# Gate and up as seven half-size products in a chain of two banks, four down groups, and TensorE's order made from two lanes

## The chip, the core and the metric

The kernel runs on one NeuronCore of a Trainium2 chip. Its engines are TensorE (PE, with the weight loads shown apart as PEld), VectorE (DVE), ScalarE (ACT), GpSimd (POOL) and SyncE (SP), which here only issues DMAs. Each engine works through its own list of instructions in order and waits at semaphores for the others. The metric is device microseconds of the whole program, from DRAM inputs to the DRAM output; lower is better.

## What is computed

A block of layer normalisation, sliding-window attention and a gated feed-forward, whose results are multiplied:

```python
xn = _layernorm(x, axis=-1)                 # x: 2048 tokens x 512
# A: 32 heads of 16, causal window of 256 tokens
qkv = xn @ wqkv; p = softmax(mask(q @ k.T * 16**-0.5)); s = (p @ v) @ wo
# B: feed-forward with F = 1792
gate = xn @ w1;  up = xn @ w3
h = silu(gate) * up
g = silu(h @ w2)
return x + s * g
```

Everything is float32. The kernel multiplies float32 as three float16 products: each operand is cut into a high half and a low half ("hi" and "lo"), and hi x hi, lo x hi and hi x lo are summed in PSUM.

## The kernel before

The 2048 tokens are four tiles `t` of 512, and the 1792 hidden features are 14 blocks `f` of 128. Attention runs in 32 units, each a tile, a group of eight heads and a half of it. A unit is split into batches: score products (`s`, in two double banks of PSUM), masks added by DVE, an exponential on ACT, row maxima for a later unit (`pass1`, on DVE, written to `junk` and `M`), and the products of probabilities and values (`po`, one double bank). These use quarter-size or half-size tiles of TensorE.

The dense work is all that uses the full 128 x 128 array: projections of Q, K and V, gate and up, down, and the output projection (`total`). It shares the last two PSUM banks, `m0` and `m1`, which `bank()` hands out in turn. `spread()` puts dense pieces between the attention batches so that TensorE always has something to do; what is left after the last unit runs at the end.

Gate and up of a block `f` of a tile (`gate_up`, L929) are 24 matmuls of 512 columns: two matrices, four chunks of the 512 features, three half products. ACT takes a tanh of the gate from its bank (L948), DVE makes `(tanh + 1) * gate` (L952) and multiplies by up (L957). Weights of gate and up are cut in tile 0, stored in DRAM as `dW1`, and loaded again for each later tile.

Down is done in groups of blocks, `GROUPS = ((0, 4), (4, 10), (10, 14))`. Tile 0 and the last group of tile 3 use plain matmuls of 512 columns (`down`, L973). The other groups are done by Strassen's scheme: with both operands cut into 2 x 2 squares, seven products of squares of half the size replace eight (`product`, L1025, matmuls of 256 columns). The sums of squares on the left are made by `lefts` (L884, POOL and ACT), those of the weights once in tile 0 (L869 to L880). Each group's result is added to a float32 sum on DVE (L1007, L1053). `combine` (L1057) makes the four result squares from the seven products on POOL. Small fixed pieces (`halves`, L312) run POOL operations as two of 256 columns.

Slots are 46 SBUF buffers handed out by `take` and `give`. Scaling of weights by powers of two is measured in tile 0 (`measure`, L784; `measure_down`, L831).

Two things set the order. TensorE's order is that in which the program is written, since `ORDERED = {ENGINE.PE}`. The other engines' order comes from `listed` (L1543 and after), a list scheduler that plays the program through with a cost for each instruction (`cost`, L1516) and a due time (`deadlines`), and then fixes the order with dependencies. The program calls `tc.manual_schedule(engines=ORDERED)`.

## Time and profile before

| | |
|---|---|
| median of 3 runs | 819.77 us (819.29 to 821.17) |
| the profiled execution | 821.13 us |
| its span, first to last instruction | 819.3 us |
| mean granted clock of TensorE | 0.994 |
| TensorE busy | 797.9 us, 97% |
| DVE busy | 639.2 us, 78% |
| ACT busy | 435.3 us, 53% |
| POOL busy | 358.7 us, 44% |
| DMA | 121.99 MB, 149 GB/s on average |

Busy time of PE is not PE at its peak: a matmul of 512 columns is shown with some 0.38 us, but the next one starts 0.216 us later. So the price of matmuls is read from start to start, that is, from the length of a long row of equal ones. Idle times are put down to the semaphore that came last. The page cuts the span into 40 slices; PE shows nine tenths or more in nearly all of them.

### The profile page before, as it was taken

To read this page: it belongs to the slowest core of one execution; us is meant where nothing else is said; L and a number is where in the kernel's file an instruction comes from. 1 tells how busy PE (TensorE), PEld (TensorE's weight loads), DVE (VectorE), ACT (ScalarE), POOL (GpSimd) and SP (SyncE) were. 2 spreads that over 40 slices of the span, in tenths; PEclk is the share of its full clock that TensorE was granted. 3 is DMA by queue.
4 is the path that set the end of the run, shared out by engine and by line. 5 is a ranking of instruction groups with operands and counts; after the bars stand their busy time and mean duration, and the time that the engine had idled before them with its cause. 6 is when DMAs were issued, how large, how long until landed. Compare 5 with 4: busy or idle time off the path is not lost.

```text
span 819.3 us, 23768 instructions
## 1 busy us (share of the span) xinstructions
PE 797.9 (97%) x9088; PEld 415.8 (51%) x9088; DVE 639.2 (78%) x2044; ACT 435.3 (53%) x659; POOL 358.7 (44%) x556
## 2 busy tenths in 40 slices
PE   8999999699999999999999999999999999999998
PEld 4444444344544554454555555545555555545654
DVE  8898889977897777799778866777878787774535
ACT  6898799555636554443443455534443446544421
POOL 2247646672806433523341752514141456435252
PEclk9999999899999999999999999999999999999999
DMA  9996575268665334545364452426375543224521
GB/s 284 284 296 185 164 215 169 75 197 204 176 179 136 117 103 121 152 144 154 106 189 133 125 142 69 140 72 172 112 185 152 159 146 113 56 90 149 172 65 55
DMA packets 112835, 121.99 MB, mean 149 GB/s; under 512 B 18448, under 2 KB 77008, under 8 KB 112720
## 3 DMA queue, kind: packets, MB, share of 16 engines
q1 hardware_dynamic: 112432, 119.94, 51.2%
q8 instruction: 71, 1.16, 0.6%
q10 hardware_dynamic: 288, 0.52, 0.2%
q14 instruction: 44, 0.36, 0.1%
HBM read 83.76 MB, written 32.37 MB: 142 GB/s over the span
## 4 chain that ended last, share of the span: by engine, by line
PE 83%; DVE 12%; issue 2%; DMA 1%; ACT 1%; DVEq 0%; SPq 0%; ACTq 0%
PE m L937 32%; PE m L1040 9%; PE m L550 9%; PE po L706 8%; PE s L678 5%; PE m L1118 5%; PE m L520 5%; PE m L987 4%; DVE junk L616 3%; PE s L604 3%; DVE s L685 2%; PE po L604 2%; DVE st L422 1%; DMA qa<-dQ 1%; DVE slot L957 1%
## 5 line engine op out<-in xcount | busy, mean ns | idle before, releaser
L688 ACT ACTIVATE pt<-s,es 128x1024 f32<-128x1024 f32 x152 | 167.7, 1113 | 198.0 <-DVE s L685 193.3
L937 PE MATMUL m<-XH,slot 128*128 128x512 f16 x896 | 267.4, 380 | 1.0 <-DVE slot L952 0.8
L316 POOL TENSOR_TENSOR slot<-slot,slot 128x256 f16<-128x256 f32 (+1 forms) x222 | 148.6, 696 | 152.4 <-ACT slot L320 66.6
L937 PEld LDWEIGHTS <-slot 128*128 128x128 f16 x1344 | 124.5, 98 | 152.6 <-issue 12.3
L937 PE MATMUL m<-XL,slot 128*128 128x512 f16 x448 | 169.8, 379 | 0.0
L685 DVE TENSOR_TENSOR s<-s,MK 128x256 f32<-128x256 f32 (+2 forms) x280 | 120.7, 437 | 50.4 <-PE s L678 41.9
L616 DVE CUSTOM_DVE_ANT_0 junk<-s,MW 128x320 bf16<-128x320 f32 x276 | 134.5, 487 | 28.0 <-PE s L604 18.6
L906 POOL TENSOR_TENSOR slot<-slot,slot 128x256 f16<-128x256 f32 x133 | 87.9, 685 | 46.4 <-ACT slot L902 46.3
L1040 PE MATMUL m<-slot,slot 128*128 128x256 f16 x798 | 96.4, 276 | 2.0 <-DVE s L685 1.8
L616 DVE CUSTOM_DVE_ANT_0 junk<-po,MW 128x320 bf16<-128x320 f32 x172 | 84.0, 488 | 10.0
L1040 PEld LDWEIGHTS <-slot 128*128 128x128 f16 x798 | 76.9, 99 | 20.4 <-issue 4.5
L706 PE MATMUL po<-pt,V 64*32 64x320 f32 (+4 forms) x2880 | 78.2, 345 | 0.0
L706 PEld LDWEIGHTS po<-pt,V 64*32 64x32 f32 x2880 | 51.9, 106 | 23.8 <-PE s L604 4.0
L910 POOL TENSOR_TENSOR slot<-slot,slot 128x256 f32<-128x256 f32 x19 | 14.2, 747 | 102.8 <-DVE slot L957 96.5
L678 PE MATMUL s<-qa,KA 50*64 50x320 f16 (+3 forms) x1472 | 58.2, 259 | 1.0 <-ACT pt L688 1.0
L987 PE MATMUL m<-slot,slot 128*128 128x512 f16 x216 | 51.6, 386 | 7.0 <-DVE slot L1007 4.7
L952 DVE SCALAR_TENSOR_TENSOR slot<-slot,m 128x512 f32<-128x512 f32 x56 | 38.3, 683 | 24.0 <-ACT slot L948 23.8
L678 PEld LDWEIGHTS <-KA 50*64 50x64 f16 x1472 | 30.2, 105 | 50.9 <-issue 36.3
L716 ACT COPY os<-po 128x512 f32<-128x512 f32 x32 | 18.7, 585 | 70.2 <-PE po L706 70.2
L948 ACT ACTIVATE slot<-m,sgs 128x512 f32<-128x512 f32 x56 | 38.3, 684 | 32.2 <-PE m L937 31.3
L957 DVE SCALAR_TENSOR_TENSOR slot<-m,slot 128x512 f32<-128x512 f32 x56 | 38.5, 687 | 15.9 <-PE m L937 15.5
L604 PE MATMUL s<-KA,qa 48*64 48x320 f16 (+2 forms) x648 | 45.5, 295 | 1.9 <-DVE M L616 0.7
(170 smaller groups left out, 1137.1 us busy)
## 6 DMA issues: line engine op xcount, KB each, us to landing
slot<-dW SPq DMA_DIRECT2D x88, 256.0 KB
slot<-dR SPq DMA_DIRECT2D x56, 256.0 KB
slot<-in_B_w_dram SPq DMA_DIRECT2D x42, 256.0 KB
dW<-slot SPq DMA_DIRECT2D x32, 256.0 KB
slot<-in_A_x_dram SPq DMA_DIRECT2D x30, 256.0 KB
KA<-dK SPq DMA_DIRECT2D x24, 288.0 KB
dR<-slot SPq DMA_DIRECT2D x49, 128.0 KB
qa<-dQ SPq DMA_DIRECT2D x32, 192.0 KB
```

Source lines behind the costliest of these rows:

```text
L316: op(out[:, c], a[:, c], b[:, c])
L550: nc.tensor.matmul(cell["pp"], a[:, k, c, :], b[:, c, :], start=(c, i) == parts[0][0], stop=(c, i) == parts[-1][-1])
L604: nc.tensor.matmul(s[64 * c:64 * c + 64, r, :n], qa[rows, 2 * p + a, ii * P + 64 * c:ii * P + 64 * c + 64], ka[rows, 2 * p + a, e - n:e], ...
L616: nc.vector.tensor_tensor_reduce(out=junk[:, :n], in0=s[:, r, :n], in1=mask, scale=1.0, scalar=NEG, op0=ALU.add, op1=ALU.max, accum_out=M[ ...
L678: nc.tensor.matmul(s[64 * h:64 * h + 64, r, o:o + 64 * n], ka[rows, 2 * p + a, 64 * (m + 4):64 * (m + 5)], qa[rows, 2 * p + a, 64 * (m + k ...
L685: nc.vector.tensor_add(v, v, MK[:, kind, of:of + n, :].unsqueeze(1).to_broadcast([P, 2 * len(which), n, 64]))
L688: nc.scalar.activation(pt, s, AF.Exp, scale=es)
L706: nc.tensor.matmul(cell["po"][32 * i:32 * i + 32, h, 64 * (m + k):64 * (m + k + n)], V[64 * h:64 * h + 64, (4 * t + m // 2) % VB, hd * VW: ...
L906: nc.gpsimd.tensor_sub(made[:, D + c.start:D + c.stop], raw[:, c], made[:, c])
L937: nc.tensor.matmul(cell[k], w[:, (a * NC + c) * P:(a * NC + c + 1) * P], b[:, c, :], start=c == 0 and i == 0, stop=c == NC - 1 and i == 2)
L987: nc.tensor.matmul(ps, hh[:, a * TW + b * P:a * TW + (b + 1) * P], w[:, c * D:(c + 1) * D], start=f == f0 and i == 0, stop=f == f1 - 1 and ...
L1040: nc.tensor.matmul(ps[:, blk, :], l[:, a * D + q:a * D + q + 128], r[:, 256 * c:256 * c + 256], start=f == f0 and x == 0, stop=f == f1 - 2 ...
```

## The change

**Gate and up of tiles 1 to 3** are done for two blocks at a time (`chain`). The weights of the pair, 512 features x 256 hidden features, and the 512 x 512 tokens of the tile are cut into 2 x 2 squares. Seven products of squares replace eight. Each is 12 matmuls of 256 columns (gate and up, two chunks, three half products) into one bank `[P, 2, 256]` that holds gate and up side by side. The seven go through two banks: `y` takes products 0, 2 and 4, and `x` takes 1, 3, 5 and 6, some of them accumulated on what is there. In between, the bank's state is taken out four times by ACT ("kept", a scaled copy into the float32 tile `cc`) and three times by DVE ("added", a scaled sum into it). The chain comes in four links of 2, 3, 1 and 1 products, and attention batches or other dense pieces are put between them; a rule in `chosen` asks for a filler before the third and the fourth link.

After a chain, tanh is taken from `cc` in SBUF, POOL multiplies gate by up (two operations a block), and one DVE operation finishes the block (`multiplied`).

**Sums of squares.** `combine_tokens` makes four sums of each later tile's tokens on POOL, cut into halves by ACT and POOL. `combine_weights` reads the weights from DRAM a second time, scales them on ACT, adds on POOL, cuts, and stores four sums per pair in `dW1`, which now holds seven squares per pair. The table `COMBOS` says at which block each pair's sums are begun: 5, 8 and 11 of tile 0, and then 0, 2, 4 and 6 of tile 1. Each product's weights (256 KB) are loaded anew, three products ahead.

**Down** has four groups, the last with two blocks. Tile 3 thus has 12 instead of 10 blocks in products. Down pieces that are due go into a list `late` and are taken off by cost (`PACE`), instead of two or three after each block.

**Room.** There are 50 slots, and the QK weights no longer stay in SBUF: they are stored in DRAM (`dWQ`) and loaded again for each later tile and group.

**Order.** TensorE is no longer in the written order. `streams` cuts its instructions into blocks of attention and of dense work (at most six matmuls), two lanes that each keep their order, and `listed` takes from the lane whose turn it is, or from the other if the first would wait more than `GAIN` = 300 ns. Costs and latencies of the scheduler are set anew, and a fault in `box` (what an access covers) is mended.

```diff
-GROUPS = ((0, 4), (4, 10), (10, 14))
+GROUPS = ((0, 4), (4, 8), (8, 12), (12, 14))
...
+CHAIN = ("12 21", "11 11", "s1 t1", "s2 t2", "s4 22", "s3 t3", "22 t4")
+WEIGHTS_AHEAD = 3
+PACE = 16
+COMBOS = {0: 5, 1: 8, 2: 11, 3: 14, 4: 16, 5: 18, 6: 20}
...
-    dW1 = dram.tile([FB, 2, P, 2 * NC * P], F16, name="dW1")
+    dWQ = [[dram.tile([P, 2 * NC * P], F16, name=f"dWQ{g}{k}") for k in range(2)] for g in range(NG)]
+    dW1 = dram.tile([FB // 2, 7, P, 2, 2, 256], F16, name="dW1")
...
+        def sums(k):
+            e, o = raws[k, 0], raws[k, 1]
+            for raw in (o, e):
+                nc.scalar.activation(raw, raw, AF.Copy, scale=pair_scale[:, j, k:k + 1])
+            nc.gpsimd.tensor_add(o[:, two], o[:, one], o[:, two])
+            nc.gpsimd.tensor_sub(o[:, one], e[:, one], o[:, one])
+            nc.gpsimd.tensor_sub(e[:, one], o[:, two], e[:, one])
+            nc.gpsimd.tensor_sub(e[:, two], e[:, two], e[:, one])
...
+    def multiplied(t, f, gate, up):
+
+        sg = take(F32)
+        nc.scalar.activation(sg, gate, AF.Tanh, scale=chain_scale[:, f // 2:f // 2 + 1])
+        halves(nc.gpsimd.tensor_mul, gate, gate, up)
+
+        def product():
+            nc.vector.scalar_tensor_tensor(sg, sg, 1.0, gate, op0=ALU.add, op1=ALU.mult)
+            WHOLE[t, f] = sg
+            finished(t, f)
+        later(1, product)
...
+        def times(p, ps, start):
+            w = WQ.pop((t, j, p))
...
+            for k in range(2):
+                for c in range(2):
+                    for i, (a, b) in enumerate(((0, 0), (1, 0), (0, 1))):
+                        first = k * 512 + a * 256 + c * P
+                        nc.tensor.matmul(ps[:, k, :], w[:, first:first + P], right[b][:, c, :],
+                                         start=start and k == 0 and c == 0 and i == 0, stop=c == 1 and i == 2, skip_group_check=True)
+            give(w)
+            fetch_weights(chains.index((t, j, p)) + 1 + WEIGHTS_AHEAD)
...
+        def kept(f, h, ps):
+            with urgent():
+                nc.scalar.activation(cell[f][:, :, 256 * h:256 * h + 256], ps, AF.Copy, scale=CS)
+
+        def added(f, h, ps):
+            c = cell[f][:, :, 256 * h:256 * h + 256]
+            with urgent():
+                nc.vector.scalar_tensor_tensor(c, ps, CS, c, op0=ALU.mult, op1=ALU.add)
...
+            times(0, cell["y"], True)
+            kept(0, 0, cell["y"])
+            times(1, cell["x"], True)
+            added(0, 0, cell["x"])
...
+            times(2, y, True)
+            kept(1, 1, y)
+            times(3, x, False)
+            times(4, y, False)
+            kept(0, 1, y)
+            added(0, 1, x)
+            done(0)
...
+            times(5, cell["x"], False)
+            added(1, 1, cell["x"])
...
+            times(6, cell["x"], False)
+            kept(1, 0, cell["x"])
+            done(1)
...
+PIECE, GAIN, LEADING, FOLLOW = 6, 300, 8000, 0.0
...
-    with _tile.TileContext(nc) as tc, tc.manual_schedule(engines=ORDERED):
+    with _tile.TileContext(nc) as tc:
```

Three places of the new order matter later. The first is DVE's list where tile 2 is normalised, in the second half of tile 0. L434 to L437 are the small steps of the reciprocal root, L440 centres the tokens, and L1007 adds a down result of tile 0 into its sum, which frees the bank `m1`. Before:

```order
L435 SCALAR_TENSOR_TENSOR sq_2852<-sq_2852,ve_2847 128x4
L436 SCALAR_TENSOR_TENSOR r0_2849<-sq_2852,r0_2849 128x4
L437 TENSOR_SCALAR rs_160<-r0_2849 128x4
L440 TENSOR_SCALAR slot9_2469<-slot9_2469,mv_159,rs_160 128x512
L440 TENSOR_SCALAR slot22_2471<-slot22_2471,mv_159,rs_160 128x512
L1007 SCALAR_TENSOR_TENSOR slot4_1423<-m1_2573,dsc_158,slot4_1423 128x512
```

After, with L1222 for the sum and L452 to L454 for the small steps:

```order
L440 BN_STATS st_3660<-slot11_3404 128x6
L440 BN_STATS st_3674<-slot30_3432 128x6
L1222 SCALAR_TENSOR_TENSOR slot35_1489<-m1_3861,dsc_170,slot35_1489 128x512
L441 BN_AGGR mv_171<-st_3660 128x2
L441 BN_AGGR mv_171<-st_3674 128x2
L445 TENSOR_SCALAR ve_3701<-mv_171 128x4
L448 TENSOR_SCALAR r0_3703<-ve_3701 128x4
L449 TENSOR_SCALAR r0_3703<-r0_3703 128x4
L452 TENSOR_TENSOR sq_3706<-r0_3703 128x4
```

The sum now stands ahead of the whole normalisation instead of behind it; five small steps later the list goes on with masks and maxima, and the rest of the steps follow between them.

The second is DVE's list at one chain of tile 1 (its sixth). L1143 is "added", L646 a row maximum, L715 a mask, L588 the low half of a projection. Before there was no such place; the nearest is a block of gate and up, of which this is the part at the end of tile 3:

```order
L685 TENSOR_TENSOR s_13215<-s_13215,MK_119 128x2x2x64
L952 SCALAR_TENSOR_TENSOR slot40_13212<-slot40_13212,m0_13199 128x512
L1125 SCALAR_TENSOR_TENSOR slot3_13245<-m1_13232,us_4300,slot39_12945 128x256
L1125 SCALAR_TENSOR_TENSOR slot3_13245<-m1_13232,us_4300,slot16_12948 128x256
L957 SCALAR_TENSOR_TENSOR slot40_13212<-m0_13251,slot40_13212 128x512
```

After:

```order
L1143 SCALAR_TENSOR_TENSOR cc_7318<-m0_7317,cc_7318 128x2x256
L715 TENSOR_TENSOR s_7457<-s_7457,MK_120 128x2x2x64
L646 ISA junk_7475,M_7294<-s_7470,MW_112 128x320
L646 ISA M_7294 128x1
L646 ISA junk_7477,M_7294<-s_7470,MW_112 128x320
```

and then, after two more maxima:

```order
L646 ISA junk_7486,M_7294<-po_7479,MW_112 128x320
L646 ISA M_7294 128x1
L588 SCALAR_TENSOR_TENSOR slot35_7452<-m1_7438,slot35_7452 128x512
L1143 SCALAR_TENSOR_TENSOR cc_7388<-m0_7317,cc_7388 128x2x256
L715 TENSOR_TENSOR s_7515<-s_7515,MK_120 128x4x64
```

The two sums that free the same bank `m0` for the chain's next products have a batch's four maxima between them.

The third is POOL's list at the very end. `combine` of tile 3 adds the seven products, which before are in slots 0, 2, 7, 24, 25, 44 and 15 and after in slots 6, 16, 21, 25, 36, 38 and 39; `on<-on,rb` divides the last attention group by its row sums, which come by DMA. Before:

```order
L316 TENSOR_TENSOR slot0_12195<-slot0_12195,slot7_11828 128x256
L316 TENSOR_TENSOR slot44_12039<-slot44_12039,slot0_12195 128x256
L316 TENSOR_TENSOR slot45_13407<-slot6_13388,slot45_13407 128x256 x2
L316 TENSOR_TENSOR slot25_12278<-slot25_12278,slot0_12195 128x256
L316 TENSOR_TENSOR on_13047<-on_13047,rb_13328 128x256 x2
L316 TENSOR_TENSOR slot4_13495<-on_13047,slot4_13495 128x256 x2
L316 TENSOR_TENSOR slot2_11811<-slot2_11811,slot44_12039 128x256
L316 TENSOR_TENSOR slot24_12058<-slot24_12058,slot44_12039 128x256 x2
```

After:

```order
L325 TENSOR_TENSOR slot38_13438<-slot38_13438,slot16_13514 128x256 x2
L325 TENSOR_TENSOR slot43_15046<-slot41_15025,slot43_15046 128x256
L325 TENSOR_TENSOR on_14610<-on_14610,rb_14983 128x256 x2
L325 TENSOR_TENSOR slot21_13631<-slot21_13631,slot16_13514 128x256
L325 TENSOR_TENSOR slot46_15208<-on_14610,slot46_15208 128x256
L325 TENSOR_TENSOR slot39_13914<-slot39_13914,slot25_13560 128x256
```

All but one of the sums now stand behind the division. On TensorE, the last seven products of tile 3 are followed at once by its 24 plain down matmuls and the output projection; before, 24 gate and up matmuls and 48 down matmuls stood there.

More of the change, by code (lines that the diff above doesn't have):

```diff
@@ L1200, in feed_forward @@
+                goal = len(pieces)
+                while late and (sum(c for c, _ in pieces[goal:]) < PACE or hasattr(pieces[-1][1], "opens")):
+                    fresh()
+                    q = late.pop(0)
+                    pieces += [q] if len(q) == 2 else products(*q)
                 for k, (f0, f1) in enumerate(GROUPS):
                     if f == f1 - 1:
-                        assert not late
-                        late = [(-1, t, k)] if halved(t, f) else [q for b in range(4) for q in down(t, k, b)]
@@ L1204, in feed_forward @@
-            if t + 2 < NT:
-                pieces.append((0, second))
-        return pieces + late
+                        late += [(-1, t, k)] if halved(t, f) else [q for b in range(4) for q in down(t, k, b)]
+        while late:
+            fresh()
+            q = late.pop(0)
+            pieces += [q] if len(q) == 2 else products(*q)
+        return pieces
     tiles = [(t, g) for t in range(NT) for g in range(NG)]
@@ L1222, in in_groups @@
         for piece in pieces:
[L1223 removed]
+            if groups and is_open(groups[-1]) and not hasattr(piece[1], "chain"):
                 groups[-1].append(piece)
```

465 lines of the change are left out of this document (349 added, 116 removed).

## The prediction

> **What bounds the kernel now.** I read the page's busy times first, then its chain of waits, then the windows, to see whether one engine holds all stages.
>
> ```profile
> span 819.3 us, 23768 instructions
> PE 797.9 (97%) x9088; PEld 415.8 (51%) x9088; DVE 639.2 (78%) x2044; ACT 435.3 (53%) x659; POOL 358.7 (44%) x556
> PE 83%; DVE 12%; issue 2%; DMA 1%; ACT 1%; DVEq 0%; SPq 0%; ACTq 0%
> 0.00:40.00 40.00, 36.10 (x202) 16.91 (x203) 32.68 (x123) 30.03 (x58) 9.39 (x39) 1.00 1.00 282
> 120.00:160.00 40.00, 32.67 (x403) 15.84 (x410) 37.26 (x126) 30.44 (x55) 25.27 (x39) 0.93 0.47 141
> 440.00:520.00 80.00, 79.79 (x1093) 45.51 (x1086) 62.53 (x197) 39.74 (x55) 36.95 (x55) 1.00 0.45 126
> ```
>
> The columns of a window are its length, the busy time of PE, PEld, DVE, ACT and POOL, the granted clock, the DMA share and GB/s. TensorE is the bound: it is busy 79.79 of 80 us in mid-kernel, DVE 62.53. The one bad stretch is 120 to 160 us: 7.3 us of PE idle and a clock of 0.93. So a matmul saved is time saved, as long as nothing else makes PE wait. The profiled execution took 821.13 us, 1.36 above the median of 819.77; I apply my sum to the median.
>
> What a matmul costs is in the chain of waits in order of time (start, length, count):
>
> ```profile
> 794.84 10.36 PE m L987 x48
> 805.20 7.77 PE m L1118 x36
> 785.62 4.04 PE m L1040 x36
> 812.97 2.63 PE m L1153 x24
> ```
>
> 512 columns cost 7.77/36 = 0.216 us, 256 columns 2.63/24 = 0.110 (4.04/36 = 0.112 over three products). Half the size is half the price, weight loads included.
>
> **PE work.** Gate and up of tiles 1 to 3 (42 blocks) are 42 x 24 = 1008 matmuls of 512 columns: 217.6 us. They become 21 chains x 7 products x 12 = 1764 of 256 columns: 193.3 us (197.9 at 0.112). Down: tile 3 has 12 blocks instead of 10 in products, so 24 large matmuls go (5.2) and 42 small ones come (4.6). **Sum -24.9 us**, between -25 and -20. The order has 165 dense stretches between attention before and 166 after, so the number of switches stays.
>
> The Trainium skill's "TensorE: Matmul & The Clock Gate", section Back-to-back issue gap, gives 81 ns at 128 columns and 131 at 512 as sustained. An estimate from it, 98 ns at 256, would make this step 1764 x 0.098 - 1008 x 0.131 = +41 us. The rows above (0.216 and 0.110) contradict that.
>
> **What comes on the other engines** (groups by form; busy, mean ns):
>
> ```profile
> L957 DVE SCALAR_TENSOR_TENSOR slot<-m,slot 128x512 f32<-128x512 f32 x56 | 38.5, 687 | 15.9 <-PE m L937 15.5
> L952 DVE SCALAR_TENSOR_TENSOR slot<-slot,m 128x512 f32<-128x512 f32 x56 | 38.3, 683 | 24.0 <-ACT slot L948 23.8
> L1053 DVE SCALAR_TENSOR_TENSOR slot<-m,dsc,slot 128x512 f32<-128x512 f32 x35 | 26.1, 746 | 11.4 <-PE m L1040 11.2
> L1093 DVE SCALAR_TENSOR_TENSOR slot<-slot,slot 128x512 f32<-128x512 f32 x12 | 8.8, 757 | 2.3 <-ACT slot L1092 2.1
> L948 ACT ACTIVATE slot<-m,sgs 128x512 f32<-128x512 f32 x56 | 38.3, 684 | 32.2 <-PE m L937 31.3 <-DMA KA<-dK 0.8
> L559 ACT ACTIVATE slot<-m 128x512 f16<-128x512 f32 x30 | 17.8, 592 | 15.6 <-PE m L550 15.4 <-DMA slot<-dW 0.2
> L319 ACT ACTIVATE slot<-slot,pi 128x512 f32<-128x512 f32 x28 | 19.8, 715 | 2.8 <-DVE pi L798 2.8
> L902 ACT CAST slot<-slot 128x512 f16<-128x512 f32 x57 | 32.9, 615 | 4.0 <-DVE slot L957 2.8 <-POOL slot L912 1.2
> L316 POOL TENSOR_TENSOR slot<-slot,slot 128x256 f16<-128x256 f32 x156 | 101.3, 678 | 102.8 <-ACT slot L320 66.6 <-ACT slot L963 33.5 <-ACT slot L877 1.6
> L316 POOL TENSOR_TENSOR slot<-slot,slot 128x256 f32<-128x256 f32 x66 | 47.3, 739 | 49.7 <-DVE slot L1125 32.6 <-DVE slot L1053 13.0 <-DVE NM L621 1.8
> ```
>
> - DVE: 42 x (0.683 + 0.687) = 57.5 goes; 63 "added" x 0.687 = 43.3 and 42 gate products x 0.757 = 31.8 come, and with four groups 21 + 4 sums x 0.746 = 18.7. +36 us: 675, 83% of some 810.
> - ACT: 42 tanh x 0.684 = 28.7 goes; 84 "kept" x 0.592, 42 tanh x 0.715, 28 scalings x 0.715 and 40 casts x 0.615 come: +96 us, 531.
> - POOL: 84 products gate x up x 0.739, weight combinations 56 x 0.739 + 56 x 0.678, token combinations 60 x 0.739 + 24 x 0.678: +202 us, 561.
>
> None passes PE in total, so they cost nothing by their sum; what hides them is PE's 795 us. The cover is thinnest on DVE, and where weights are combined early: ACT has 9.6 us free from 120 to 160, POOL 14.7, and one pair wants 4 x 0.715 + 4 x 0.615 = 5.3 of ACT and 11.3 of POOL. Exponentials delayed there cost 0 to 8 us; combinations are ordered by need and the first chain comes two units later, so I take +1. SP issues 1090 DMAs instead of 901, for 63 more weight loads and 24 reloads of the QK weights (23 MB). Over t = 1 to 3 that is some 40 GB/s on top of 126, where 282 was reached in the first 40 us. With weights asked for three products (3.9 us) ahead I take 0.
>
> **The opening stall.** In the timeline (start, length; the bracket is idle time and what ended it):
>
> ```profile
> 150.11 0.65 DVE L434 TENSOR_TENSOR sq<-r 128x4 f32<-128x4 f32 x1
> 150.70 3.17 POOL L316 TENSOR_TENSOR slot<-slot,slot 128x256 f16<-128x256 f32 x5
> 155.05 0.75 DVE L1007 SCALAR_TENSOR_TENSOR slot<-m,dsc,slot 128x512 f32<-128x512 f32 x1
> 155.85 2.72 PE L987 MATMUL m<-slot,slot 128*128 128x512 f16 x6 [4.66 <-DVE slot L1007]
> 369.70 0.16 DVE L434 TENSOR_TENSOR sq<-r 128x4 f32<-128x4 f32 x1
> ```
>
> PE waits 4.66 us for the sum L1007, which stands on DVE behind the whole normalisation of tile 2: small steps of 0.65 us while POOL works, 0.16 while it doesn't. Afterwards six matmuls take 2.72 instead of 1.3 us. In the new order the sum stands ahead of that normalisation, whose steps are split by masks and maxima, and the second group needs weights of 4 blocks instead of 6. I take the 4.66, 1.4 of slow clock and 0.6 of the short waits before: **-6.7 us** (0 if another stall replaces it, -8.7 with all 7.3 idle and the 1.4).
>
> **Waits inside a chain.** A chain holds both dense banks, so each next product waits for an evacuation.
>
> ```profile
> 792.28 0.69 ACT L948 ACTIVATE slot<-m,sgs 128x512 f32<-128x512 f32 x1 [6.04 <-PE m L937]
> 793.00 0.69 DVE L952 SCALAR_TENSOR_TENSOR slot<-slot,m 128x512 f32<-128x512 f32 x1 [1.04 <-ACT slot L948]
> 366.30 0.38 PE L550 MATMUL m<-XL,whi 128*128 128x512 f16 x1
> 366.77 0.60 ACT L559 ACTIVATE slot<-m 128x512 f16<-128x512 f32 x1 [2.61 <-PE m L550]
> 368.72 0.67 DVE L563 SCALAR_TENSOR_TENSOR slot<-m,slot 128x512 f16<-128x512 f32 x1
> 369.44 0.38 PE L520 MATMUL m<-wvh,XH 128*128 128x512 f16 x1 [0.79 <-DVE slot L563]
> 308.70 0.64 PE L678 MATMUL s<-qa,KA 50*64 50x320 f16 x24
> 309.41 1.90 PE L1118 MATMUL m<-slot,slot 128*128 128x512 f16 x8
> ```
>
> Hops: PE to ACT 366.77 - 366.30 - 0.22 = 0.25, ACT to DVE 0.03, DVE to PE 0.05. The fifth to the sixth product (kept, then added) needs 0.25 + 0.59 + 0.03 + 0.69 + 0.05 = 1.6 us, sixth to seventh (added) 1.0, third to fifth 0.9 against 1.3 of the product between. An attention block covers 0.7 at most (308.70 to 309.41). By the new order 18 of 21 chains have a dense piece or the value products at the first place; three have only such a block: 3 x 0.9. At the second place eight have only a block (0.5 on average) and the last has nothing: 8 x 0.5 + 1.0. That is 8 us. It is the floor: L563 above could have run at 367.4 and ran at 368.72, behind four maxima, 1.35 us late. If that befalls one link of each chain it is 28 more. At most places ACT and DVE are as free as in mid-kernel, so I stay near the floor: **+13 us** (8 to 36).
>
> **The tail.**
>
> ```profile
> 783.07 2.55 PE L706 MATMUL po<-pt,V 64*32 64x256 f32 x96
> 789.70 0.75 DVE L1053 SCALAR_TENSOR_TENSOR slot<-m,dsc,slot 128x512 f32<-128x512 f32 x1 [1.21 <-PE m L1040]
> 790.53 4.38 POOL L316 TENSOR_TENSOR slot<-slot,slot 128x256 f32<-128x256 f32 x6 [0.43 <-DVE slot L1053]
> 797.54 0.88 DVE L1007 SCALAR_TENSOR_TENSOR slot<-m,dsc,slot 128x256 f32<-128x256 f32 x2 [1.98 <-PE m L987]
> 800.08 1.41 POOL L316 TENSOR_TENSOR on<-on,rb 128x256 f32<-128x256 f32 x2 [0.85 <-DMA rb<-de]
> ```
>
> Before, POOL's sums of the seven products (6 in 4.38 us) run under 24 gate/up and 12 down matmuls, until 797.54. After, down follows the products at once, and POOL's order puts on<-on,rb ahead of those sums. It waits for a DMA and started 14.5 us after the last values (785.6 to 800.1). The new products end 1.0 + 2.6 + 9.2 = 12.8 us after the values, so POOL starts it 1.7 us later; then come 1.4, and six half operations of about 0.72 to the first complete pair of sums, six more to the second. The sum of the third down block ends some 12.5 us after the products, and the output projection that reuses its bank could have begun at 24 x 0.216 = 5.2: +7.4, and some slow clock after the idle: **+8 us** (0 to 10).
>
> **Sum:** -24.9 - 6.7 + 13 + 8 + 1 = -9.6: 819.77 becomes **810**. About 0.2% (1.6 us) can be told from no change here.
>
> **Rivals.**
> 1. Everything covered: the chains at their floor of 8, and the tail's DMA landing early: -24.9 - 6.7 + 8 + 2 = -22, 798. For it speaks that PE waits for almost nothing in mid-kernel now; against it DVE at 83%.
> 2. Bank waits decide, slower. If each chain waits 1.35 us at one more link, chains cost 36. PE stalls also cost clock:
>
> ```profile
> 750.88 5.77 PE L1040 MATMUL m<-slot,slot 128*128 128x256 f16 x36 [1.79 <-DVE s L685]
> ```
>
> After 1.79 us of idle the next 36 matmuls took 5.77 instead of 4.04 us, 1.7 lost. With that at five chains it is 36 + 8.5: -24.9 - 6.7 + 44.5 + 8 + 1 = +22, 842. It turns slower once chains cost over 23 us, 1.1 each. The Trainium skill states this mechanism ("TensorE: Matmul & The Clock Gate", section A second HAM failure mode): cycling PSUM banks makes PE idle briefly so often that its clock keeps falling. This trace shows the fall twice, each after a stall of 1.8 us or more.
> 3. The gain eaten exactly: 820.
>
> **Chances:** forecast (803 to 817) 0.45, rival 1 0.27, rival 2 0.23, rival 3 0.05. Faster 0.72, same 0.05, slower 0.23. The range reaches from 792 (rival 1 with 6 us of attention waits gone) to 832 (between forecast and rival 2).
>
> **What would show it.** The chain matmuls at 0.110 us start to start; no DVE wait of 4 us before down of tile 0; idle before the chain matmuls, ended by ACT or DVE writing cc, near 13 us; some 7 us of idle before down and output projection at the end, with POOL waiting for rb<-de. I am wrong if DVE's queue holds evacuations in every chain, or if half-speed clock stretches number more than five.

## The result, and the profile after

The changed kernel takes **868.69 us** (median of 4 runs, 866.57 to 869.13), against 820.38 for the kernel before in the same job. The ratio is 1.0585, with a 95% interval of 1.0562 to 1.0607. The prediction was 810 us, range 792 to 832. Sign and size were both wrong.

The page of the profiled execution (869.13 us):

```profile
span 867.3 us, 26240 instructions
PE 796.2 (92%) x9888; PEld 500.5 (58%) x9888; DVE 697.6 (80%) x2115; ACT 514.9 (59%) x813; POOL 558.8 (64%) x843
PE 45%; DVE 22%; POOL 10%; DMA 8%; issue 6%; ACT 5%; SPq 3%; POOLq 0%; DVEq 0%; ACTq 0%
```

ACT and POOL came out close to the estimates (531 and 561). DVE did not: it is busy for 58 us more than before, where +36 (675) was expected; run 13 below shows what the rest is. TensorE's own busy time fell by 1.7 us instead of 24.9, and the rest of the span, in which it is not busy, grew from 21.4 to 71.1 us. The chain of waits now runs through PE for 45% of the span; before, it was 83%. So TensorE alone no longer sets the time: PE, DVE, POOL and DMA hand the end to each other.

The windows show where. The columns are those of the windows in the prediction. Two rows of the kernel before that are not shown there:

```profile
160.00:200.00 40.00, 39.99 (x446) 18.84 (x432) 30.17 (x106) 19.39 (x29) 21.76 (x33) 0.99 0.65 177
280.00:360.00 80.00, 79.66 (x978) 40.30 (x977) 62.56 (x198) 40.81 (x56) 32.03 (x46) 1.00 0.49 138
```

The changed kernel:

```profile
120.00:160.00 40.00, 37.64 (x533) 19.63 (x533) 34.87 (x126) 33.43 (x60) 37.32 (x58) 1.00 0.76 208
160.00:200.00 40.00, 35.66 (x331) 16.09 (x329) 34.72 (x110) 28.24 (x47) 31.67 (x49) 0.91 0.65 161
280.00:360.00 80.00, 70.17 (x973) 47.69 (x979) 57.74 (x169) 54.60 (x86) 69.40 (x103) 0.96 0.74 212
440.00:520.00 80.00, 74.82 (x1085) 52.59 (x1083) 72.10 (x202) 37.75 (x54) 44.38 (x64) 0.98 0.60 170
```

TensorE loses some 10 of 80 us at 280 to 360, where POOL is busy for 69.4 of 80, and 5 at 440 to 520. The opening did not become better: 6.7 us of idle from 120 to 200 instead of 7.3, and the clock is down there again.

Groups of TensorE instructions by line; the last part of each row is the idle time just before them and what ended it:

```profile
L1131 PE MATMUL m<-slot,slot 128*128 128x256 f16 x1008 | 124.1, 277 | 11.4 <-DVE cc L1143 10.9 <-ACT cc L1138 0.2
L1255 PE MATMUL m<-slot,slot 128*128 128x256 f16 x840 | 102.1, 275 | 7.3 <-DMA on<-os 4.0 <-DVE slot L1268 3.3
L1131 PE MATMUL m<-XH,slot 128*128 128x256 f16 x504 | 86.4, 275 | 7.1 <-ACT cc L1138 3.2 <-DMA slot<-dW 1.7 <-DVE slot L1340 1.1
L708 PE MATMUL s<-qa,KA 50*64 50x320 f16 (+3 forms) x1472 | 59.8, 261 | 16.4 <-ACT pt L718 10.7 <-DVE M L646 3.4 <-issue 0.8
L634 PE MATMUL s<-KA,qa 48*64 48x320 f16 (+2 forms) x648 | 48.3, 303 | 9.4 <-DVE M L646 3.5 <-DVE mt L667 2.5 <-ACT pt L718 1.4
```

The two attention lines of the kernel before:

```profile
L678 PE MATMUL s<-qa,KA 50*64 50x320 f16 (+3 forms) x1472 | 58.2, 259 | 1.0 <-ACT pt L688 1.0
L604 PE MATMUL s<-KA,qa 48*64 48x320 f16 (+2 forms) x648 | 45.5, 295 | 1.9 <-DVE M L616 0.7 <-DMA qa<-dQ 0.5 <-ACT pt L688 0.4
```

The chains wait 14.3 us for `cc` (10.9 + 0.2 + 3.2), that is, for evacuations: the steps of ACT and DVE that take a bank's state out. They are 16 waits, the longest of 2.3 us. Attention, which the change does not touch, waits 25.8 us instead of 2.9, for exponentials and row maxima.

The price of a matmul is as predicted, except where the clock is down. From the chain of waits in order of time:

```profile
406.97 2.73 PE m L1131 x24
449.92 2.72 PE m L1131 x12
474.88 4.04 PE m L1131 x36
```

36 take 4.04 us, 0.112 each. The 12 at 449.92 take as long as 24 elsewhere: they follow a wait of 2.34 us. The mean clock is 0.978, before 0.994. In the stretches of the clock record with a granted clock of 0.50 TensorE is busy for 30.2 us, before for 8.1; half of that is lost, 15.1 us against 4.1, so 11 more. A second part is the ends of rows. TensorE is stopped 112 times instead of 34, and 33 of the 78 further stops come after dense work, whose last matmul is shown with some 0.165 us more than its step to the next (0.275 against 0.110 us at 256 columns). That is about 5 us, an estimate. With 24.9 saved, 11 lost to the clock and 5 at these ends, some 7 of the 23 missing us of busy time are not placed.

**Why an evacuation is late.** The same place in the timeline:

```profile
444.80 1.47 PE L1131 MATMUL m<-slot,slot 128*128 128x256 f16 x12 [0.65 <-DVE cc L1143]
...
447.77 0.90 DVE L461 TENSOR_SCALAR slot<-slot,mv,rs 128x512 f32<-128x512 f32 x1
448.59 0.68 DVE L588 SCALAR_TENSOR_TENSOR slot<-m,slot 128x512 f16<-128x512 f32 x1
449.20 0.67 DVE L1143 SCALAR_TENSOR_TENSOR cc<-m,cc 128x512 f32<-128x512 f32 x1
...
449.92 1.44 PE L1131 MATMUL m<-slot,slot 128*128 128x256 f16 x6 [2.34 <-DVE cc L1143]
```

The products end at 446.3. DVE is then in a row of maxima, a centring and the low half of a projection, and starts the sum at 449.20, 2.9 us late. The sum itself takes 0.67.

**How POOL reaches TensorE.** At 296 us, filtered to one thread of waits:

```profile
296.03 1.41 POOL L325 TENSOR_TENSOR cc<-cc 128x256 f32<-128x256 f32 x2
...
297.47 1.14 DVE L1007 SCALAR_TENSOR_TENSOR slot<-slot,cc 128x512 f32<-128x512 f32 x1 [2.18 <-POOL cc L325]
...
298.70 0.60 ACT L1138 ACTIVATE cc<-m 128x512 f32<-128x512 f32 x1 [3.62 <-DVE slot L1007]
...
299.35 0.38 PE L1131 MATMUL m<-XH,slot 128*128 128x256 f16 x2 [1.85 <-ACT cc L1138]
```

There are two `cc` buffers (`cpool` has two). POOL's gate x up is late; DVE's product waits for it; ACT can't evacuate the next chain's first bank, because its `cc` buffer still holds that block; TensorE waits for the bank.

**DVE shut out.** And this at 160 us, POOL and DVE and then TensorE:

```profile
157.38 5.08 POOL L325 TENSOR_TENSOR slot<-slot,slot 128x256 f16<-128x256 f32 x8
159.71 5.96 DVE L651 TENSOR_SCALAR NM<-M 128x16 f16<-128x16 f32 x1
...
164.92 0.73 POOL L873 TENSOR_TENSOR slot<-slot 128x256 f32<-128x256 f32 x1
165.73 0.72 POOL L874 TENSOR_TENSOR slot<-slot,slot 128x256 f32<-128x256 f32 x1
165.93 0.25 PE L634 MATMUL s<-KA,qa 48*64 48x128 f16 x4 [2.09 <-DVE M L646]
```

A step of 128x16, whose median is 0.49 us here and 0.18 in the kernel before, stands for 5.96. POOL runs without a pause from before it until 164.92 + 0.73 = 165.65, and the step ends at 165.67, in the first gap between two POOL instructions. The same happens at 709.61 (5.19 us), and TensorE then waits 3.36. These are the only two such steps in this kernel.

### The profile page after: what moved, and what is told of

Same layout as the page of the kernel before. It is cut to its first block, busy times and chain, and to the rows that moved or that the text cites. A ratio compares the mean times of both kernels' runs of the same rounds, so it can differ in the third digit from the quotient of the medians.

```text
span 867.3 us, 26240 instructions
## 1 busy us (share of the span) xinstructions
PE 796.2 (92%) x9888; PEld 500.5 (58%) x9888; DVE 697.6 (80%) x2115; ACT 514.9 (59%) x813; POOL 558.8 (64%) x843
## 2 busy tenths in 40 slices
DMA packets 163358, 159.76 MB, mean 184 GB/s; under 512 B 21472, under 2 KB 118560, under 8 KB 163232
## 4 chain that ended last, share of the span: by engine, by line
PE 45%; DVE 22%; POOL 10%; DMA 8%; issue 6%; ACT 5%; SPq 3%; POOLq 0%; DVEq 0%; ACTq 0%
PE m L1131 14%; PE m L1255 7%; DVE junk L646 6%; POOL slot L325 5%; PE po L737 5%; PE m L573 4%; DVE s L715 3%; PE s L708 3%; PE m L1333 2%; PE m L542 2%; PE m L1038 2%; ACT pt L718 2%; PE s L634 2%; SPq L781 2%; DMA slot<-dW 2%
## 5 line engine op out<-in xcount | busy, mean ns | idle before, releaser
L325 POOL TENSOR_TENSOR slot<-slot,slot 128x256 f16<-128x256 f32 (+1 forms) x298 | 203.4, 712 | 88.8 <-DMA slot<-in_B_w_dram 30.4
L1131 PEld LDWEIGHTS <-slot 128*128 128x128 f16 x1764 | 169.5, 99 | 55.1 <-issue 26.6
L646 DVE CUSTOM_DVE_ANT_0 junk<-s,MW 128x320 bf16<-128x320 f32 x276 | 134.0, 486 | 34.6 <-PE s L634 23.0
L715 DVE TENSOR_TENSOR s<-s,MK 128x256 f32<-128x256 f32 (+2 forms) x280 | 120.0, 434 | 36.2 <-PE s L708 27.3
L1131 PE MATMUL m<-slot,slot 128*128 128x256 f16 x1008 | 124.1, 277 | 11.4 <-DVE cc L1143 10.9
L325 POOL TENSOR_TENSOR cc<-cc 128x256 f32<-128x256 f32 x84 | 61.0, 748 | 85.7 <-ACT slot L1003 59.4
L1255 PE MATMUL m<-slot,slot 128*128 128x256 f16 x840 | 102.1, 275 | 7.3 <-DMA on<-os 4.0
L980 POOL TENSOR_TENSOR slot<-slot,slot 128x256 f16<-128x256 f32 x140 | 92.1, 680 | 15.6 <-ACT slot L976 15.5
L1255 PEld LDWEIGHTS <-slot 128*128 128x128 f16 x840 | 79.9, 98 | 24.2 <-issue 12.1
L1131 PE MATMUL m<-XH,slot 128*128 128x256 f16 x504 | 86.4, 275 | 7.1 <-ACT cc L1138 3.2
L646 DVE CUSTOM_DVE_ANT_0 junk<-po,MW 128x320 bf16<-128x320 f32 x172 | 83.7, 487 | 9.2 <-DVE M L646 0.5
L1038 PE MATMUL m<-XH,slot 128*128 128x512 f16 x224 | 69.8, 394 | 3.6 <-DVE slot L1052 1.9
L1138 ACT ACTIVATE cc<-m 128x512 f32<-128x512 f32 x84 | 49.9, 594 | 36.7 <-PE m L1131 30.7
L573 PE MATMUL m<-XH,slot 128*128 128x512 f16 x240 | 70.8, 379 | 0.7 <-DVE slot L1268 0.4
L1131 PE MATMUL m<-XL,slot 128*128 128x256 f16 x252 | 69.3, 275 | 0.0
L708 PEld LDWEIGHTS <-KA 50*64 50x64 f16 x1472 | 32.2, 106 | 55.6 <-issue 44.1
L573 PEld LDWEIGHTS <-slot 128*128 128x128 f16 x384 | 36.8, 98 | 42.1 <-issue 1.5
L1038 PEld LDWEIGHTS <-slot 128*128 128x128 f16 x336 | 32.4, 101 | 44.9 <-issue 8.6
```

Of the source, the lines that this page charges most:

```text
L325: op(out[:, c], a[:, c], b[:, c])
L573: nc.tensor.matmul(cell["pp"], a[:, k, c, :], b[:, c, :], start=(c, i) == parts[0][0], stop=(c, i) == parts[-1][-1])
L646: nc.vector.tensor_tensor_reduce(out=junk[:, :n], in0=s[:, r, :n], in1=mask, scale=1.0, scalar=NEG, op0=ALU.add, op1=ALU.max, accum_out=M[ ...
L708: nc.tensor.matmul(s[64 * h:64 * h + 64, r, o:o + 64 * n], ka[rows, 2 * p + a, 64 * (m + 4):64 * (m + 5)], qa[rows, 2 * p + a, 64 * (m + k ...
L715: nc.vector.tensor_add(v, v, MK[:, kind, of:of + n, :].unsqueeze(1).to_broadcast([P, 2 * len(which), n, 64]))
L980: nc.gpsimd.tensor_sub(made[:, D + c.start:D + c.stop], raw[:, c], made[:, c])
```

## The experiments

All ratios are against the kernel before, run in the same job. Runs 3, 5 to 8, 12, 14, 16 and 18 leave work out or put constants in its place, so their values are not those of the block. "Side work" is what prepares and follows the chains: the weight sums, the token sums and gate x up.

One thing bears on all comparisons. The planner orders the engines anew for every edit. Only runs 13, 14 and 15 have the order of the kernel that they are compared with (13 with the changed kernel, 14 with 12, 15 with the kernel before). In run 10, where one number of the planner was changed and no instruction, some 85% of DVE's steps stand in the changed kernel's order, and its single times reach from 862.97 to 874.27 us. So differences of a few us between other runs can be the plan's own.

Three theories at first. A: the new planner and TensorE's two lanes delay attention. B: POOL's 200 us of new work delays DVE and with it attention. C: the evacuations hold the chains' banks.

**1. The new planner alone, on the old kernel.** The functions from `arrange` on are taken from the changed kernel, and `manual_schedule` is left out; all else is as before.

> The kernel before with one part of the change alone: the new planner (the new durations, and TensorE in two lanes) orders the old gate/up, the old three down groups and the old combinations. Theory A (the new order of TensorE makes attention wait): 840 to 865 us, with 20 us or more of TensorE idle that ends with maxima or exponentials. Theory B (GpSimd's 200 us of new work slows DVE's small steps, and attention with them) and theory C (the banks of the chains): 815 to 823, as before.

830.85 us, ratio 1.0129 (1.0073 to 1.0185). The planner alone costs about 10 us, less than A expected and more than B and C did.

**2. The changed kernel in the written order of TensorE.**

```diff
-PIECE, GAIN, LEADING, FOLLOW = 6, 300, 8000, 0.0
+PIECE, GAIN, LEADING, FOLLOW = 6, 300, -1, 0.0
```

> The changed kernel, with TensorE kept in the order in which the program is written (the second lane may never lead). Theory A: the time falls to 830 to 850. Theory B: 865 to 880, since the same work stands on GpSimd and DVE. Theory C: 875 to 900, since nothing is pulled ahead to cover a bank that is being read.

876.77 us, 1.0688 (1.0647 to 1.0730). The two lanes help by 8 us here, so they are not the cause, and A falls as the main one. B and C both allow the number.

**3. POOL relieved.**

```diff
-        halves(nc.gpsimd.tensor_mul, gate, gate, up)
...
-            nc.gpsimd.tensor_add(o[:, two], o[:, one], o[:, two])
-            nc.gpsimd.tensor_sub(o[:, one], e[:, one], o[:, one])
-            nc.gpsimd.tensor_sub(e[:, one], o[:, two], e[:, one])
-            nc.gpsimd.tensor_sub(e[:, two], e[:, two], e[:, one])
...
-            halves(nc.gpsimd.tensor_sub, made[:, D:], raw, made[:, 0:D])
+            nc.gpsimd.memset(made[:, D:].bitcast(F32), 0.0)
```

> The changed kernel with GpSimd relieved: left out are gate x up, the four sums of a weight pair and the sums of the token halves; the low halves of the combined weights and tokens are filled with zeros instead of a subtraction. Some 170 of GpSimd's 559 us go. Everything on TensorE, all evacuations on ACT and DVE and all DMAs stay. Theory B: 820 to 840, with the smallest DVE steps (the doubled maxima, 0.73 us now) back near 0.3. Theories A and C: 860 to 869.

The sums of the token halves are left out as well and filled by `memset`. 850.70 us, 1.0376 (1.0356 to 1.0395): 18 of 48 us come back, less than B expected, and the scaling of the maxima (L651) still takes 466 ns on average where some 300 were expected. B holds in part.

**4. POOL loaded, in the old kernel.** After each block of tiles 1 to 3:

```diff
+                for _ in range(3 * (t > 0)):
+                    for c in range(2):
+                        nc.gpsimd.tensor_add(load_pool, sg[:, 256 * c:256 * c + 256], sg[:, 256 * c:256 * c + 256])
```

> The kernel before with 252 additions on GpSimd put in, six half additions after each gate/up block of tiles 1 to 3, which nothing reads: 252 x 0.739 = 186 us more on GpSimd. Theory B: 835 to 860, with the small DVE steps at 0.5 us or more. Theories A and C: 819 to 824.

835.69 us, 1.0190 (1.0173 to 1.0207). The time is at B's lower edge, but B's sign is missing: the scaling of the maxima takes as long as in the kernel before (280 ns), not 500 or more.

```profile
L621 DVE TENSOR_SCALAR NM<-M 128x16 f16<-128x16 f32 x32 | 9.0, 280 | 0.8
```

The place does not fit either:

```profile
280.00:360.00 80.00, 79.66 (x914) 41.02 (x912) 61.40 (x190) 41.11 (x57) 59.17 (x91) 1.00 0.48 125
```

With POOL busy for 59 of 80 us instead of 32, TensorE stays at 79.66. From 200 to 760 us this kernel loses 3 us of TensorE's busy time in all; the rest of its loss lies before and after. In mid-kernel the load by itself costs the old kernel next to nothing. In the changed one POOL's result stands on the way to a `cc` buffer; that this is why it costs there is argued from the thread above, not tried by itself.

**5 and 6. The bank held for a short time**, with all side work and with POOL relieved:

```diff
-                nc.scalar.activation(cell[f][:, :, 256 * h:256 * h + 256], ps, AF.Copy, scale=CS)
+                nc.scalar.activation(cell[f][:, :, 256 * h:256 * h + 16], ps[:, :, 0:16], AF.Copy, scale=CS)
+                nc.scalar.activation(cell[f][:, :, 256 * h + 15:256 * h + 256], filler, AF.Copy, scale=CS)
```

and the same for the sum on DVE.

> The changed kernel, in which each evacuation of a chain reads 16 of 256 columns from the bank and fills the other 241 from a constant in a second instruction, so a bank is held for a small instruction in place of 0.59 us (ACT) or 0.69 (DVE); ACT and DVE do the same work and a little more, and nearly all values are wrong. Theory C (banks held by evacuations): the 15 us of idle blamed on cc go, and clock and drains with them: 838 to 850. If what counts is the load on DVE and ACT or the late attention: 862 to 875.

> The short hold of the bank together with the relieved GpSimd of the earlier run (gate x up, weight sums and token sums left out). If the two causes add up, 18 us for GpSimd and 20 to 30 for the banks: 815 to 832. If there is a third cause of more than 20 us (the new TensorE order, DMA, the scalings on ACT): 840 to 852.

869.22 us (1.0610, 1.0576 to 1.0644) and 841.85 (1.0282, 1.0249 to 1.0314). With all side work the short hold gains nothing, although a bank is now freed by an instruction of 0.18 to 0.19 us instead of 0.59 or 0.69: the chains wait 14.5 us for `cc`, against 14.3. With POOL relieved it gains 8 to 9 us. C falls in this form for the full kernel: an evacuation is late because of what stands ahead of it in its queue, more than because it is long. (ACT and DVE are busy for 16 and 11 us more here than in the changed kernel.)

**7 and 8. One kind of side work out at a time**: no combination of weights (the plain cut weights are stored in their place), and no gate x up.

> The changed kernel without any combination of gate and up weights: no second load of the raw weights, no scaling and casting on ACT, no sums on GpSimd; the plain cut weights are stored once more in their place, so TensorE and the DMAs of the chains are as before and the values are wrong. Theory D (this burst between 100 and 330 us delays the exponentials and the evacuations): 838 to 852, with the gain nearly all before 360 us. Otherwise 860 to 869.

> The changed kernel without the 84 half products gate x up on GpSimd (61 us), so that DVE's product follows the tanh directly; values of tiles 1 to 3 are wrong. If GpSimd's share of the loss lies here: 850 to 858, with the gain spread from 240 us to the end. If it lies in the weight sums: 864 to 870.

844.61 us (1.0308, 1.0290 to 1.0325) and 848.51 (1.0343, 1.0314 to 1.0372). Run 7 gives back 24 us (POOL's and ACT's work and the second load), run 8 20, and run 3, which took POOL's part of both away, 18. The parts do not add up, and run 3 even gains less than run 8, which leaves out less of POOL's work. That they fill the same slack would explain the first; the second may be the plan.

**9 to 11. Two suspects by name**: the shut-out step moved to ACT, and SyncE's issues planned slower.

```diff
-                nc.vector.tensor_scalar(nm[:, 0, :], Mf, -1.0 / ONE, None, op0=ALU.mult)
+                nc.scalar.activation(nm[:, 0, :], Mf, AF.Copy, scale=-1.0 / ONE)
...
-            return 340
+            return 470
```

> The changed kernel with one instruction per attention unit moved from DVE to ACT: the 128x16 scaling of the maxima, which in the changed kernel twice lasted 5.2 to 6.0 us (at 159.7 and 709.6 us) until a run of GpSimd instructions ended. Theory F (DVE is shut out by runs of GpSimd instructions, and TensorE waits and loses clock behind it): both stalls go, with 5.4 us of idle and 8.5 us of work lost to the half clock after them, 850 to 860. If those stalls are covered elsewhere: 864 to 872.

> The changed kernel, the same instructions, with one number of the planner changed: a DMA issue is planned at 470 ns in place of 340, since the trace has one each 0.46 to 0.54 us. Theory E (SyncE falls behind its plan between 120 and 440 us, and ACT, DVE and GpSimd stand with a late load at the head of their queues): 845 to 858, with less slip before 440 us. If the queue is not what delays them: 864 to 874.

> Both edits, the scaling of the maxima on ACT and DMA issues planned at 470 ns. If E and F are separate causes: 832 to 848. If they are one: as the better of the two. If neither holds: 864 to 874.

867.71 us (1.0565, 1.0516 to 1.0613), 873.50 (1.0599, 1.0530 to 1.0669) and 866.22 (1.0553, 1.0522 to 1.0584). None helps: run 10's own time is 4.8 us longer, and all three intervals overlap the changed kernel's. In run 9 the shut-outs moved to other small steps and are five instead of two; the longest:

```profile
205.20 7.40 DVE L445 TENSOR_SCALAR ve<-mv 128x4 f32<-128x4 f32 x1
```

**12. The bare chain**: all three kinds of side work out.

> The changed kernel with all new side work out at once: no combination of weights (neither loads nor scalings nor sums), no gate x up on GpSimd, and the sums of token halves replaced by fills; TensorE, the chains' bank evacuations, the tanh and the products on DVE stay, and the values are wrong. GpSimd is then about as busy as before the change. If the side work is the whole loss and the chains themselves keep their gain: 798 to 815. If the chains themselves (half-size products, two banks held, more evacuations) eat the gain: 828 to 842.

840.33 us, 1.0232 (1.0169 to 1.0294). The side work costs 28 us, but without it the chains still lose: 840 where 25 us of TensorE's work are saved. POOL is at 44%, as before, and here too DVE is shut out, four times: a step of 128x32 lasted 4.42 us at 478.50.

**13 to 15. POOL paced.** Every engine keeps its instructions and their order; each POOL instruction waits for the one before.

```diff
-                              mybir.DependencyInfo(mybir.DependencyClass.NoSync, mybir.DependencyReason.DATA), reason="order")
+                              mybir.DependencyInfo(mybir.DependencyClass.Sync if e == ENGINE.Pool else mybir.DependencyClass.NoSync, mybir.DependencyReason.DATA), reason="order")
```

> The changed kernel with the same instructions in the same order on every engine; each GpSimd instruction now waits until the one before it has ended (until now only those that read or overwrite its result did), which leaves some 0.1 us between any two. Theory F (runs of GpSimd instructions without such a pause shut DVE's small steps out for 2 to 7 us, and TensorE waits and loses clock behind them): no DVE step over 1.5 us longer than usual, and 840 to 856. If the shut-out steps cost TensorE nothing in sum, or the slower GpSimd (some 60 us more) costs as much: 866 to 885.

> The bare chain of the earlier run (840.3 us), with GpSimd's instructions paced in the same way. Theory F: its four shut-outs (2.6 to 4.7 us) go, 820 to 832. Otherwise 838 to 848.

> The kernel before with GpSimd's instructions paced in the same way. Its longest delay of a DVE step is 0.56 us, so by theory F nothing is to be gained: 817 to 823. If the pauses themselves cost: 824 to 832.

871.73 us (1.0644, 1.0611 to 1.0678), 833.92 (1.0174, 1.0159 to 1.0189) and 820.57 (1.0013, 1.0004 to 1.0023). The shut-outs are gone: in run 13 no DVE step lasts more than 0.6 us over the shortest of its kind. The changed kernel's scaling of the maxima, which was

```profile
L651 DVE TENSOR_SCALAR NM<-M 128x16 f16<-128x16 f32 x32 | 23.4, 732 | 0.5
```

is now

```profile
L651 DVE TENSOR_SCALAR NM<-M 128x16 f16<-128x16 f32 x32 | 10.9, 341 | 0.5
```

Of the 12.5 us between the two rows some 11 are the two steps of 5.96 and 5.19. All of DVE is busy for 670.9 us instead of 697.6, close to the 675 of the prediction, so what it had above the estimate was time in which it stood still for POOL. In the bare chain pacing is worth 6 us (all four times of run 14 lie below all four of run 12, but the two intervals overlap, and 833.92 lies between the two expectations). In the full kernel the gain is given back between 200 and 360 us, where the paced POOL is later still with gate x up:

```profile
280.00:360.00 80.00, 65.50 (x827) 43.64 (x812) 51.17 (x157) 49.48 (x77) 67.43 (x94) 0.94 0.65 184
```

TensorE is busy for 65.50 us there instead of 70.17. One product waits 5.20 us, by the same thread of waits through ACT, DVE and POOL as above:

```profile
298.95 0.58 PE L1131 MATMUL m<-XH,slot 128*128 128x256 f16 x2 [5.20 <-ACT cc L1138]
```

**16. The bare, paced chain with the short hold.**

> The bare chain with paced GpSimd (833.9 us), and with the short hold of the bank as in the earlier run with all its side work (16 of 256 columns read from the bank, the rest filled; values wrong). If the hold of the two banks is what is left of the chains' cost, its 11 us of idle blamed on cc go: 818 to 826. If an evacuation is late because it stands in a queue, however short it is: 830 to 838.

831.54 us, 1.0150 (1.0128 to 1.0172): 2 us, inside the second expectation, and no more than a new plan can make.

**17. Gate x up on DVE.**

```diff
-        halves(nc.gpsimd.tensor_mul, gate, gate, up)
+        nc.vector.tensor_mul(gate, gate, up)
```

> The changed kernel with gate x up moved from GpSimd (84 halves, 61 us) to DVE (42 whole products, some 25 to 33 us), all values right. If GpSimd is the engine that is too full between 200 and 440 us: 850 to 860, near the run that left the product out (848.5). If DVE has no room for it: 866 to 880.

873.84 us, 1.0649 (1.0621 to 1.0676), inside the second expectation: nothing is gained by moving it to DVE, which is then busy for 716 us.

**18. The bare, paced chain with DVE relieved**: the sums touch 16 of 256 columns.

```diff
-                nc.vector.scalar_tensor_tensor(c, ps, CS, c, op0=ALU.mult, op1=ALU.add)
+                nc.vector.scalar_tensor_tensor(c[:, :, 0:16], ps[:, :, 0:16], CS, c[:, :, 0:16], op0=ALU.mult, op1=ALU.add)
```

> The bare chain with paced GpSimd (833.9 us), in which the 63 additions of a bank on DVE read and write only 16 of 256 columns and nothing fills the rest (values wrong): some 35 us of DVE's 658 go, so that it has less to do than in the kernel before (639), and the banks it reads come free sooner. If what is left of the chains' cost is DVE's queue: 815 to 825. If it is the fixed order of chain and attention, whatever the load: 829 to 834.

823.90 us, 1.0042 (1.0025 to 1.0059). With some 29 us of DVE's work gone the kernel is 10 us faster, inside the first expectation; DVE's busy time, 628.8, is below that of the kernel before. The shorter hold of the bank is part of the edit, but run 16 had that too and gained 2. The chain products now wait 3.1 us for DVE instead of 9.8 in run 14. Run 14, and then run 18:

```profile
L1094 PE MATMUL m<-slot,slot 128*128 128x256 f16 x1008 | 123.3, 276 | 9.9 <-DVE cc L1106 9.8
```

```profile
L1094 PE MATMUL m<-slot,slot 128*128 128x256 f16 x1008 | 121.1, 273 | 3.4 <-DVE cc L1106 3.1 <-ACT cc L1101 0.2
L708 PE MATMUL s<-qa,KA 50*64 50x320 f16 (+3 forms) x1472 | 58.4, 259 | 7.7 <-ACT pt L718 4.5 <-DVE mt L667 2.0 <-DVE XL L510 0.6
```

**What follows.** The ladder is 869 (all), 840 (without side work), 834 (no shut-outs), 824 (less on DVE), and 820 is the kernel before. The side work is 28 us of it, far outside the noise and what a new plan was seen to make; the two smaller steps are less sure, for the reasons given with them. That they cost so much because they stand between two products of a chain, or ahead of attention in the same queue, is read from the threads above.

The ladder does not reach the ground. With 24.9 us of TensorE's work saved, 820 would become 795; the last step, 824, is 29 us above that. Of these, about 16 are idle time (37.7 us in run 18, 21.4 in the kernel before) and 12 are busy time that did not go. What holds it there is not settled. The planner alone costs the old kernel some 10 us (run 1), but whether it costs the chains as much was not tried. The runs that leave work out multiply other numbers; whether that touches the clock was not tried either. No version beat the kernel before.

## Why the prediction was wrong, point by point

- **PE work, -24.9.** The price per matmul held (0.112 us). The step failed in that the saving did not stay on TensorE: its busy time fell by 1.7, with some 11 us lost to the clock, which the sum had not counted outside the opening and the tail, and some 5 at the ends of rows, for which it had no term.
- **"None passes PE in total, so they cost nothing by their sum", +1 (0 to 8).** This is the step that decided. Leaving the new side work out gives 28 us back (run 12), far outside its bounds. The total itself was too small for DVE: +58 us instead of +36, since it stood still for POOL (run 13). A total says that the work fits, not that each piece is done when its reader comes. The thread POOL, DVE, `cc`, ACT, TensorE could have been read from the diff: two `cc` buffers, each held until POOL and DVE are done with it.
- **Waits inside a chain, +13 (8 to 36).** The size was right, 14.3 us, but in part by luck. The floor in it was made of hops and of evacuation times, waits of 0.5 to 1.0 us; in fact the place in the queue counts. There are 16 waits of up to 2.3 us, and evacuations of 16 columns made TensorE wait as long as those of 256 (14.5 us in run 5).
- **Attention.** The sum had no term for it but the +1 for exponentials early on. It waits 23 us more (25.8 against 2.9), which makes it the largest piece of the new idle time. Chains and attention share DVE's and ACT's queues, and what makes a chain's bank wait makes a batch wait too.
- **Opening stall, -6.7.** The named wait is gone as predicted, but others took its place (6.7 us of idle from 120 to 200 us, against 7.3). Its bound of 0 was the right end.
- **DMA, 0.** TensorE waits 5.7 us for DMAs (`on<-os` 4.0, `slot<-dW` 1.7), and the traffic grew by 38 MB (159.76 against 121.99), not by 23. Planning the issues slower did not help (run 10).
- **Tail, +8.** The waits at the end, in the timeline:

```profile
837.09 6.71 PE L1255 MATMUL m<-slot,slot 128*128 128x256 f16 x60 [2.60 <-DVE slot L1268]
849.89 7.92 PE L1333 MATMUL m<-slot,slot 128*128 128x512 f16 x35 [0.91 <-DVE slot L1222]
859.86 1.48 PE L1368 MATMUL m<-slot,slot 128*128 128x256 f16 x12 [1.28 <-DVE slot L1340]
```

  2.60 + 0.91 + 1.28 = 4.8 us, inside 0 to 10. The thread that I had named is there but small: POOL waits 3.98 us for `rb<-de` until 845.82, its sums follow the division, DVE waits for one of them until 849.35, and TensorE gets its bank 0.91 us late, where 7.4 were forecast. The largest wait, 2.60, is another: DVE stands from 831.8 on a reciprocal that needs the DMA `dr<-dd` (4.35 us, until 836.12), and the sum that frees the bank (L1268) stands behind it in the queue.
- **The rivals.** Rival 2 (842, chance 0.23) had the sign, and part of the mechanism: bank waits, and clock lost after idle time. The Trainium skill's "TensorE: Matmul & The Clock Gate", section A second HAM failure mode, says that short idles between groups of matmuls make the clock fall again and again. The mean clock of 0.978 instead of 0.994, and 12 matmuls in 2.72 us at 449.92, agree. But that is the only fall here that follows a wait for a chain's bank. The others stand at waits for the first normalisation (2.09 us, until 12.73), for maxima behind the two shut-outs (2.09, until 165.93, and 3.36, until 716.60), for an exponential (3.00, until 218.47) and for a DMA (3.81, until 322.49). What rival 2 lacked is the side work and attention. The sign I had set for being wrong, more than five half-speed stretches, was met: the clock record shows six ahead of the end.
- **The planner.** I counted its new costs and lanes as nothing; alone they cost the old kernel 10 us.

## What to carry to other kernels

When an engine at 97% is relieved by work moved to others, price each moved piece by its place: who reads it, what stands ahead of it in its in-order queue, and which buffer it holds until then; a busy share of 60 to 80% is no cover for a result that must come within 1 us. A scheme of half-size products also halves the time in which the other bank must be emptied (12 matmuls last 1.3 us instead of 2.6). Leave the support work out in a run of its own: here it cost 28 us, more than the 25 that the scheme could save. Where a planner orders every version anew, also change one of its numbers with the same instructions, so as to see how much the plan alone moves.

## What the runs showed of the hardware

- **A run of POOL instructions can shut a small DVE step out until it ends.** Up to 7.40 us for a step of 128x4 (run 9) and 4.42 us for one of 128x32 (run 12), each ending within 0.05 us of the end of POOL's unbroken row. It is rare. In the changed kernel 315 small steps began with 1.5 us or more of such a row ahead: 252 were hardly delayed, 61 by 0.15 to 1 us, and two to the end of the row. In run 9 it is five of 287, in run 12 four of 152, in the kernel before none of 129. What sets these few apart was not found. The row of eight at 157.38 shows why there is no gap: 5.08 us for eight is 0.635 from start to start, while the group's mean duration is 0.68 to 0.70, so that each starts before the last has ended. Making each wait for the one before (run 13) took all of these away. The Trainium skill's "SBUF — State Buffer", section Who interferes with whom, says that DVE and GpSimd share a pair of ports under an exclusive lock that is held for an instruction. The delays below 1 us, about one POOL instruction, agree. That a step can also wait for several in a row is what these runs add; that the lock then passes from one POOL instruction to the next would explain it, and is not shown by itself.
- **Pauses on POOL cost little where POOL is not full.** In the old kernel, with POOL at 46%, they moved the time by 0.13% (0.04 to 0.23).
- **The clock can fall at a single wait of some 2 us.** After 2.34 us of idle at 449.92, 12 matmuls of 256 columns took 2.72 us, 0.227 each, twice the price of the 36 at 474.88. It need not: of the eleven waits of 1.8 us or more in the changed kernel, four (2.02 us until 120.28, 1.85 until 299.35, 1.83 until 303.36, 2.60 until 837.09) have no half-speed stretch with them.
